# Cosine attention with a gated two-product tail: squares and norms of the next pairs reordered, one activation table load, weights in four transfers, both products of a batch in one phase

## The chip, the cores and the metric

One core of a Trainium2 chip. The time is device microseconds of one launch, the median of several runs; the profile is one execution of the same program, and its span is 1.7 to 1.8 us shorter than the time of that execution.

## The reference, cut to what matters

```python
# q, k, v: (8, 12, 448, 64) fp32; w_in (768, 2048), w_out (2048, 768)
q_n = q / (norm(q) + 1e-6);  k_n = k / (norm(k) + 1e-6)
attn = softmax(q_n @ k_n.T / tau)
x = (attn @ v) laid out as (8 * 448, 768)        # heads side by side
h = x @ w_in
g = h * clip(h + 3, 0, 6) / 6
out = g @ w_out                                  # (3584, 768) fp32
```

## The kernel before: the parts that matter

Heads are worked in 48 pairs, six pairs to a batch. A stretch of six pairs, from slot 2 of pair 6 on, is called a phase: in it the products of finished batches are spread between the attention of the next. A unit, or block, is a group of matmuls into one PSUM bank, up to its eviction, the copy that empties the bank. Each pair has four slots; in a slot TensorE computes scores of two key blocks (one in slot 3), ScalarE takes the exponential, and other work is placed between. The order in this text is the order on each engine's queue.

```python
def norms(i):                          # before: reduction and norms together
    nc.vector.tensor_reduce(out=n2, in_=sq, ...)            # 14 sums of 64 squares
    nc.scalar.activation(out=ln, in_=n2, func=AF.Ln)        # four steps of 128x14
    nc.scalar.activation(out=nr, in_=ln, func=AF.Exp, scale=0.5)
    nc.scalar.activation(out=le, in_=nr, func=AF.Ln, bias=eps_bias)
    nc.scalar.activation(out=r, in_=le, func=AF.Exp, scale=-1.0)

def mm1_unit(b, fc):                   # one block of x @ w_in: 6 matmuls of 448 columns
    ...                                # then ScalarE: u = relu(h/6 + 0.5); VectorE: g = min(u, 1) * h
def mm2_unit(b, t, m):                 # one block of g @ w_out: 16 matmuls of 384 columns
    ...                                # then one copy and the store
def back(i):                           # transposes of a pair's output into Z, VectorE copies Z to xT
    ...
def transposes(i):                     # transposes of normalised q and k into the same Z,
    ...                                # VectorE copies them to qT and kz

def add_batch(b):                      # w_in of batch b, interleaved with w_out of batch b-1
    first = [mm1_unit(b, fc) for fc in range(16)] if b < B else []
    second = [mm2_unit(b - 1, t, m) ...] if b > 0 else []
    ...

for i in range(48):
    for s in range(4):
        if i % 6 == 0 and i > 0 and s == 2:
            add_batch(i // 6 - 1)      # from here six pairs' worth of slots to spread it over
        scores(i, s, SC2 if i < 6 and s % 2 else SC)        # and their exponential
        if s == 0:
            load(...)                  # q, k, v of two pairs
            square(i + 3, nc.gpsimd); normalise(i + 2, nc.gpsimd); vcast(i + 2, nc.gpsimd)
            next_weights()             # one of eight transfers, GpSimd's queue, fp32 to bf16
            fill(0.6 * ns); values(i - 1, 3); finish_values(i - 1); fill(0.4 * ns)
        elif s == 1:
            fill(0.8 * ns); back(i - 1); norms(i + 3); fill(0.2 * ns)
        elif s == 2:
            fill(0.4 * ns); transposes(i + 1); fill(0.6 * ns); values(i, 0); values(i, 1)
        else:
            fill(ns); values(i, 2)
...
add_batch(B - 1); add_batch(B); fill(1e9)      # the tail: w_in of batch 7, w_out of 6 and 7
```

`fill` hands TensorE about that much time of the stream of w_in and w_out units. From pair 6 on, one bank pair (SC) serves all four slots, so the scores of a slot wait for the exponential of the slot before.

Of the kernel before, what the change touches and what calls it, by code (L numbers as in the profile page):

```python
# [8 lines left out]
FP32 = mybir.dt.float32  # L9
BF16 = mybir.dt.bfloat16  # L10
AF = mybir.ActivationFunctionType
ALU = mybir.AluOpType
# [3 lines left out]
MM1_NS = 190.0  # L16
# [4 lines left out]
def kernel(  # L21
# [54 lines left out]
    raw_of, nrm_of, r_of, qT_of, at_of, on_of = {}, {}, {}, {}, {}, {}  # L76


    def load(d, n_pairs=2, first=0, engs=None):

        b, h = 2 * d // HP, 4 * d % H + 2 * first
        if first == 0:
            raw_of[d] = sb.tile([128, 4, 7, D], FP32, name="raw", tag="raw", bufs=3)
        raw = raw_of[d][:, 2 * first : 2 * (first + n_pairs), :, :]
        vt = vr[d % NV][:, 2 * first : 2 * (first + n_pairs), :, :]
        hs = slice(h, h + 2 * n_pairs)
        e0, e1 = engs or (nc.sync, nc.sync)

        def main(t):
            return t[b, hs, 0:SM, :].rearrange("h (p c) d -> p h c d", c=3)  # L90


        for n, t in enumerate((k, q) if b % 2 else (q, k)):
            e0.dma_start(out=raw[:, :, 4 * n : 4 * n + 3, :], in_=main(t))
            e1.dma_start(  # L95
                out=raw[64 * n : 64 * n + 64, :, 3, :],
                in_=t[b, hs, SM:S, :].rearrange("h p d -> p h d"),
            )
        e1.dma_start(out=vt[:, :, 0:3, :], in_=main(v))
        for g in range(2):  # L100
            e0.dma_start(
                out=vt[64 * g : 64 * g + 64, :, 3, :].rearrange("p (i g) d -> p i g d", g=2)[:, :, g, :],
                in_=v[b, hs, SM:S, :].rearrange("(i g) p d -> p i g d", g=2)[:, :, g, :],
            )
# [4 lines left out]
    def square(i, eng):  # L109
        sq = sb.tile([128, 2, 7, D], FP32, name="sq", tag="sq", bufs=2)  # L110
        r_of[i] = sq
        a = raw_pair(i)
        if eng is None:
            nc.scalar.activation(out=sq[:, :, 0:3, :], in_=a[:, :, 0:3, :], func=AF.Square)
            nc.vector.tensor_tensor(
                out=sq[:, :, 3:7, :], in0=a[:, :, 3:7, :], in1=a[:, :, 3:7, :], op=ALU.mult
            )
        else:
            eng.tensor_tensor(out=sq[:, :, :, :], in0=a, in1=a, op=ALU.mult)  # L119

    def norms(i):

        sq = r_of[i]
        n2 = sb.tile([128, 14], FP32, name="n2", tag="n2", bufs=2)
# [4 lines left out]
        nc.vector.tensor_reduce(  # L129
            out=n2[:, :], in_=sq[:, :, :, :].rearrange("p h s d -> p (h s) d"), axis=AX.X, op=ALU.add  # L130
        )
# [191 lines left out]
    def add_batch(b):  # L323

        first = [mm1_unit(b, fc) for fc in range(FCN)] if b < B else []
        second = []
        if b > 0:
            p = b - 1
            second = [mm2_unit(p, t, m) for t in range(3 + p % 2) for m in range(2)]
        stream_ns[0] += len(first) * CC * MM1_NS + len(second) * FCN * MM2_NS  # L330
        done = 0
        for n, u in enumerate(first):
            stream.append(u)
            while second and done * len(first) < (n + 1) * (6 + 2 * ((b - 1) % 2)) - len(first):
                stream.append(second.pop(0))
                done += 1
        stream.extend(second)
# [5 lines left out]
    load(0, 1, 0, (nc.sync, nc.scalar))  # L343
    load(0, 1, 1, (nc.sync, nc.scalar))
    nc.scalar.preload_act_table_set("natural_log_exp_and_others")
    load(1)
    load(2)
# [3 lines left out]
    nc.gpsimd.memset(kz[0][:, :, :], 0.0)  # L351
    for t in vx:
# [4 lines left out]
    nc.gpsimd.memset(kz[1][:, :, :], 0.0)  # L357

    FG = d_ff // 4
    weights = [  # L360
        (w_in_sb[:, :, f * FG : (f + 1) * FG], w_in_r[:, :, f * FG : (f + 1) * FG]) for f in range(4)
    ] + [(w_out_sb[:, 4 * f : 4 * f + 4, :], w_out_r[:, 4 * f : 4 * f + 4, :]) for f in range(4)]

    def next_weights():
        if weights:
            o, w = weights.pop(0)
            nc.gpsimd.dma_start(out=o, in_=w)

    square(0, None)
    norms(0)  # L370
    square(1, nc.vector)
    normalise(0, nc.vector)
    vcast(0, nc.gpsimd)
    norms(1)
    transposes(0)
    normalise(1, nc.vector)
    square(2, nc.gpsimd)
    vcast(1, nc.gpsimd)
    next_weights()
    norms(2)  # L380
# [8 lines left out]
    for i in range(NP):  # L389
# [7 lines left out]
        for s in range(4):  # L397
# [6 lines left out]
            if s == 0:  # L404
                if i % 2 and (i + 5) // 2 < NP // 2:
                    load((i + 5) // 2)
                if i + 3 < NP:
                    square(i + 3, nc.gpsimd)
                if i + 2 < NP:
                    normalise(i + 2, nc.gpsimd)  # L410
                    vcast(i + 2, nc.gpsimd)
                next_weights()
# [5 lines left out]
            elif s == 1:  # L418
                fill(0.8 * ns)
                if i > 0:  # L420
                    back(i - 1)
                if i + 3 < NP:
                    norms(i + 3)
                fill(0.2 * ns)
            elif s == 2:
                fill(0.4 * ns)
# [5 lines left out]
            else:  # L432
                fill(ns)
# [7 lines left out]
    add_batch(B)  # L441
# [36 lines left out]
```

## Time and profile before

| | before |
|---|---|
| median of runs | 510.05 us (509.06 to 512.22) |
| profiled span | 509.7 us, last matmul ends 505.3 |
| exponential of pair 0, slot 0 | 17.39 us |
| exponential of pair 6, slot 2 (start of the stream) | 56.41 us |
| TensorE stalls from there on (see below) | 38.6 us |

In profile lines PE is TensorE, PEld its weight loads, ACT ScalarE, DVE VectorE, POOL GpSimd, SPq and the like the queues that issue transfers. A line of a timeline has start and length in us, engine, line of the kernel and operation; what stands in brackets is how long the engine had been idle and who ended that. SC is the bank pair of the scores, M and Y banks of the products, Z the one bank of all transposes.

A stall here is the start of a matmul less the start of the one before it and that one's streaming time, where over 0.06 us. The page of the profile, parts 2 and 4: busy tenths of 40 equal slices, and the engines' shares of the chain of work that ended last.

```profile
PE   0666767779999999999999999999999999999996
DMA  7999994210432504514432505514431000010022
PE 60%; ACT 15%; DVE 10%; DMA 7%; SPq 4%; issue 2%; POOL 1%; ACTq 0%; POOLq 0%
```

TensorE is below 80% in the first nine slices, DMA at 90% or more in slices two to six; 40% of the chain is not TensorE. The waits, in the form "engine, tile and line waited for whom: us in total, times, longest":

```profile
ACT ln L132 <- DVE n L129: 86.8, 48, 4.4
PE SC L184 <- ACT at L188: 28.4, 36, 3.4
PE Z L154 <- DVE xT L241: 1.7, 3, 0.7
```

The first norm step waits for the reduction in every one of 48 pairs, 86.8 us in total; score products wait for exponentials, 28.4 us.

### The profile page before, as it was taken

To read this page: it belongs to the slowest core of one execution; us is meant where nothing else is said; L and a number is where in the kernel's file an instruction comes from. 1 tells how busy PE (TensorE), PEld (TensorE's weight loads), DVE (VectorE), ACT (ScalarE), POOL (GpSimd) and SP (SyncE) were. 2 spreads that over 40 slices of the span, in tenths; PEclk is the share of its full clock that TensorE was granted. 3 is DMA by queue.
4 is the path that set the end of the run, shared out by engine and by line. 5 is a ranking of instruction groups with operands and counts; after the bars stand their busy time and mean duration, and the time that the engine had idled before them with its cause. 6 is when DMAs were issued, how large, how long until landed. Compare 5 with 4: busy or idle time off the path is not lost.

```text
span 509.7 us, 9679 instructions
## 1 busy us (share of the span) xinstructions
PE 449.6 (88%) x3872; PEld 274.9 (54%) x3872; DVE 259.3 (51%) x568; ACT 282.5 (55%) x543; POOL 189.3 (37%) x156
## 2 busy tenths in 40 slices
PE   0666767779999999999999999999999999999996
PEld 0343434445555656655555656655555656655563
DVE  5665545554645555554645555545645454433310
ACT  3566646666566655566566655566565655533300
POOL 2996275444344343344354343344353320000000
PEclk9988989999999999999999999999999999999999
DMA  7999994210432504514432505514431000010022
GB/s 211 251 221 221 239 221 110 68 41 17 125 97 60 140 15 140 140 39 120 125 90 66 141 18 139 141 36 120 125 107 50 32 27 21 32 48 32 31 78 63
DMA packets 71581, 50.96 MB, mean 100 GB/s; under 512 B 22384, under 2 KB 71536, under 8 KB 71536
## 3 DMA queue, kind: packets, MB, share of 16 engines
q1 hardware_dynamic: 65168, 43.53, 31.5%
q0 software_dynamic: 5248, 6.29, 7.0%
q8 instruction: 30, 0.49, 0.4%
q10 hardware_dynamic: 1120, 0.52, 0.4%
q14 instruction: 15, 0.12, 0.1%
HBM read 45.61 MB, written 11.01 MB: 111 GB/s over the span
## 4 chain that ended last, share of the span: by engine, by line
PE 60%; ACT 15%; DVE 10%; DMA 7%; SPq 4%; issue 2%; POOL 1%; ACTq 0%; POOLq 0%
PE M L286 17%; PE M L257 13%; PE SC L184 9%; PE Y L286 8%; ACT at L188 7%; PE Y L257 7%; DVE n L129 6%; DMA raw<-in_q_dram 5%; PE PV L214 4%; ACT le L134 2%; DVE xT L241 2%; PE Z L240 2%; SPq L95 1%; ACT u L267 1%; ACT nr L133 1%
## 5 line engine op out<-in xcount | busy, mean ns | idle before, releaser
L188 ACT ACTIVATE at<-SC 128x896 bf16<-128x896 f32 x192 | 156.4, 820 | 65.2 <-PE SC L184 63.7
L141 POOL TENSOR_TENSOR nrm<-raw,r 128x896 bf16<-128x896 f32 x46 | 77.6, 1687 | 206.9 <-ACT r L135 196.5
L184 PE MATMUL SC<-qT,kz 128*128 128x448 bf16 x336 | 97.9, 363 | 29.7 <-ACT at L188 28.4
L257 PE MATMUL M<-xT,w_in_sb 128*128 128x448 bf16 x510 | 120.8, 353 | 0.0
L286 PE MATMUL M<-w_out_sb,gT 128*128 128x384 bf16 x608 | 118.1, 326 | 0.0
L286 PEld LDWEIGHTS <-gT 128*128 128x128 bf16 x896 | 84.5, 98 | 60.2 <-issue 5.2
L257 PEld LDWEIGHTS <-w_in_sb 128*128 128x128 bf16 x768 | 72.5, 98 | 77.3 <-issue 22.1
L270 DVE SCALAR_TENSOR_TENSOR gT<-u,M 128x448 bf16<-128x448 bf16 x85 | 52.7, 621 | 98.3 <-ACT u L267 97.9
L119 POOL TENSOR_TENSOR sq<-raw 128x896 f32<-128x896 f32 x46 | 77.3, 1680 | 18.7 <-DMA raw<-in_q_dram 12.2
L214 PEld LDWEIGHTS <-at 128*128 128x128 bf16 x1344 | 64.0, 99 | 30.8 <-ACT at L188 9.3
L214 PE MATMUL PV<-vx,at 128*128 128x65 bf16 (+1 forms) x1344 | 71.7, 199 | 7.0 <-ACT at L188 6.9
L267 ACT ACTIVATE u<-M,half_bias 128x448 bf16<-128x448 f32 x85 | 53.4, 630 | 22.6 <-PE M L257 22.3
L257 PE MATMUL Y<-xT,w_in_sb 128*128 128x448 bf16 x258 | 63.1, 355 | 0.0
L132 ACT ACTIVATE ln<-n 128x14 f32<-128x14 f32 x48 | 10.3, 215 | 86.8 <-DVE n L129 86.8
L286 PE MATMUL Y<-w_out_sb,gT 128*128 128x384 bf16 x288 | 56.7, 326 | 0.0
L129 DVE TENSOR_REDUCE n<-sq 128x14 f32<-128x896 f32 x48 | 51.6, 1076 | 6.7 <-POOL sq L119 4.5
L270 DVE SCALAR_TENSOR_TENSOR gT<-u,Y 128x448 bf16<-128x448 bf16 x43 | 26.7, 621 | 46.3 <-ACT u L267 45.9
L184 PEld LDWEIGHTS <-kz 128*128 128x128 bf16 x336 | 29.7, 99 | 21.3 <-issue 7.9
L154 PE MATMUL Z<-ident,nrm 128*128 128x128 bf16 x336 | 27.9, 225 | 13.4 <-DVE nrm L141 11.4
L154 PEld LDWEIGHTS <-nrm 128*128 128x128 bf16 x336 | 23.9, 101 | 23.5 <-DVE nrm L141 11.4
L229 DVE TENSOR_TENSOR on<-PV,rc 128x512 bf16<-128x512 f32 x48 | 33.2, 691 | 1.7
L241 DVE COPY xT<-Z 128x448 bf16<-128x448 bf16 x48 | 18.7, 389 | 29.1 <-PE Z L240 29.1
(44 smaller groups left out, 244.7 us busy)
## 6 DMA issues: line engine op xcount, KB each, us to landing
out_dram<-o SPq DMA_DIRECT2D x48, 192.0 KB, 1.9
raw<-in_q_dram SPq DMA_DIRECT2D x23, 384.0 KB, 5.1
raw<-in_k_dram SPq DMA_DIRECT2D x23, 384.0 KB, 5.2
vr<-in_v_dram SPq DMA_DIRECT2D x23, 384.0 KB, 5.5
w_in_sb<-in_moe_w_in_dram POOLq DMA_DIRECT2D x4, 768.0 KB, 11.7
w_out_sb<-in_moe_w_out_dram POOLq DMA_DIRECT2D x4, 768.0 KB, 12.2
out_dram<-o SPq DMA_DIRECT2D x16, 96.0 KB, 2.2
raw<-in_q_dram SPq DMA_DIRECT2D x23, 64.0 KB, 4.8
```

The lines of the kernel that those rows point to most:

```text
L119: eng.tensor_tensor(out=sq[:, :, :, :], in0=a, in1=a, op=ALU.mult)
L129: nc.vector.tensor_reduce(out=n2[:, :], in_=sq[:, :, :, :].rearrange("p h s d -> p (h s) d"), axis=AX.X, op=ALU.add)
L141: eng.tensor_tensor(out=nrm[:, :, :, :].rearrange("p s h d -> p h s d"), in0=raw_pair(i), in1=r_of[i][:, :].rearrange("p (h s) -> p h s", ...
L154: nc.tensor.transpose(Z[:, s * 128 : (s + 1) * 128], nrm[:, s, :, :], ident[:, :])
L184: nc.tensor.matmul(sc[:, n, 0:S], k_block(i, name), qT_of[i][:, :], start=True, stop=True)
L188: nc.scalar.activation(out=at[:, 0:m, :], in_=sc[:, 0:m, 0:S], func=AF.Exp, scale=inv_tau)
L214: nc.tensor.matmul(o, at[:, n, q_cols(i // HP, j)], mv, start=(name == "A0" and j % 2 == 0), stop=last, skip_group_check=True,)
L229: nc.vector.tensor_tensor(out=on[:, :, :, :].rearrange("p (b j) h d -> p b (j h) d", b=2), in0=pv4[:, :, :, 0:D], in1=rc[:, :, :].to_broad ...
L257: nc.tensor.matmul(ps[:, 0:S], w_in_sb[:, cc, fc * 128 : (fc + 1) * 128], x[:, cc, c0 : c0 + S], start=(cc == 0), stop=(cc == CC - 1),)
L267: nc.scalar.activation(out=u[:, :], in_=ps[:, 0:S], func=AF.Relu, bias=half_bias[:, :], scale=1.0 / 6.0)
L270: nc.vector.scalar_tensor_tensor(out=g[:, fc, c0 : c0 + S], in0=u[:, :], scalar=1.0, in1=ps[:, 0:S], op0=ALU.min, op1=ALU.mult,)
L286: nc.tensor.matmul(ps[:, 0:MH], lhs, w_out_sb[:, fc, m * MH : (m + 1) * MH], start=(fc == 0), stop=(fc == FCN - 1),)
```

## The change

Its intent: take the norms out of the way by preparing them a slot earlier, start the first pairs sooner (squares shared with ScalarE, loads of q and k ahead of v, no second table load), use fewer weight transfers, and fill the first phase, which had no w_out products. Core of the diff, cut:

```diff
-    def norms(i):                     # reduction and four steps
+    def reduce(i): ...                # the reduction alone
+    def norms(i): ...                 # the four steps alone
...
     def add_batch(b):
-        first = [mm1_unit(b, fc) for fc in range(FCN)] if b < B else []
-        ...                           # w_out of b - 1 interleaved
+        for fc in range(FCN):
+            stream.append(mm1_unit(b, fc))
+        for t in range(3 + b % 2):
+            for m in range(2):
+                stream.append(mm2_unit(b, t, m))
...
-    nc.scalar.preload_act_table_set("natural_log_exp_and_others")   # the second one
-    load(1); load(2)
+    load_qk(1); load_v(0); load_qk(2); load_v(1); load_v(2)
...
-    weights = [4 quarters of w_in] + [4 quarters of w_out]
+    weights = [2 halves of w_in] + [2 halves of w_out]
...
             if s == 0:
-                square(i + 3, nc.gpsimd); normalise(i + 2, ...); vcast(i + 2, ...)
-                next_weights()
             elif s == 1:
+                norms(i + 2)
                 fill(0.8 * ns)
                 back(i - 1)
-                norms(i + 3)
             elif s == 2:
+                square(i + 3, 3 if i < HP else 0, nc.gpsimd)   # 3 of 7 blocks on ScalarE
+                normalise(i + 2, ...); vcast(i + 2, ...)
+                if i in (0, 3, 5): next_weights()
             else:
+                reduce(i + 3)
...
-    add_batch(B - 1); add_batch(B)
+    add_batch(B - 1)
```

More of the change, by code (lines that the diff above doesn't have):

```diff
@@ L74, with load_qk @@
     moe_banks = [Y]
-    raw_of, nrm_of, r_of, qT_of, at_of, on_of = {}, {}, {}, {}, {}, {}
-    def load(d, n_pairs=2, first=0, engs=None):
+    raw_of, sq_of, n2_of, nrm_of, r_of, qT_of, at_of, on_of = {}, {}, {}, {}, {}, {}, {}, {}
+    def load_qk(d, first=0, n_pairs=2, e0=nc.sync, e1=nc.sync):
         b, h = 2 * d // HP, 4 * d % H + 2 * first
@@ L84, in load @@
         raw = raw_of[d][:, 2 * first : 2 * (first + n_pairs), :, :]
-        vt = vr[d % NV][:, 2 * first : 2 * (first + n_pairs), :, :]
         hs = slice(h, h + 2 * n_pairs)
-        e0, e1 = engs or (nc.sync, nc.sync)
-        def main(t):
-            return t[b, hs, 0:SM, :].rearrange("h (p c) d -> p h c d", c=3)
         for n, t in enumerate((k, q) if b % 2 else (q, k)):
-            e0.dma_start(out=raw[:, :, 4 * n : 4 * n + 3, :], in_=main(t))
+            e0.dma_start(
+                out=raw[:, :, 4 * n : 4 * n + 3, :],
+                in_=t[b, hs, 0:SM, :].rearrange("h (p c) d -> p h c d", c=3),
+            )
             e1.dma_start(
@@ L98, in load, with load_v @@
             )
-        e1.dma_start(out=vt[:, :, 0:3, :], in_=main(v))
+    def load_v(d):
+        b, h = 2 * d // HP, 4 * d % H
+        vt, vs = vr[d % NV], v[b, h : h + 4]
+        nc.sync.dma_start(
+            out=vt[:, :, 0:3, :], in_=vs[:, 0:SM, :].rearrange("h (p c) d -> p h c d", c=3)
+        )
         for g in range(2):
-            e0.dma_start(
-                out=vt[64 * g : 64 * g + 64, :, 3, :].rearrange("p (i g) d -> p i g d", g=2)[:, :, g, :],
-                in_=v[b, hs, SM:S, :].rearrange("(i g) p d -> p i g d", g=2)[:, :, g, :],
+            nc.sync.dma_start(
+                out=vt[64 * g : 64 * g + 64, g:4:2, 3, :],
+                in_=vs[g:4:2, SM:S, :].rearrange("h p d -> p h d"),
             )
@@ L107, in raw_pair, with square, reduce @@
         return raw_of[i // 2][:, 2 * (i % 2) : 2 * (i % 2) + 2, :, :]
-    def square(i, eng):
+    def square(i, n_act, eng):
         sq = sb.tile([128, 2, 7, D], FP32, name="sq", tag="sq", bufs=2)
-        r_of[i] = sq
+        sq_of[i] = sq
         a = raw_pair(i)
-        if eng is None:
-            nc.scalar.activation(out=sq[:, :, 0:3, :], in_=a[:, :, 0:3, :], func=AF.Square)
-            nc.vector.tensor_tensor(
-                out=sq[:, :, 3:7, :], in0=a[:, :, 3:7, :], in1=a[:, :, 3:7, :], op=ALU.mult
-            )
-        else:
-            eng.tensor_tensor(out=sq[:, :, :, :], in0=a, in1=a, op=ALU.mult)
+        if n_act:
+            nc.scalar.activation(
+                out=sq[:, :, 0:n_act, :], in_=a[:, :, 0:n_act, :], func=AF.Square
+            )
+        if n_act < 7:
+            eng.tensor_tensor(
+                out=sq[:, :, n_act:7, :], in0=a[:, :, n_act:7, :], in1=a[:, :, n_act:7, :], op=ALU.mult
+            )
+    def reduce(i):
+        n2 = sb.tile([128, 14], FP32, name="n2", tag="n2", bufs=3)
+        n2_of[i] = n2
+        nc.vector.tensor_reduce(
+            out=n2[:, :],
+            in_=sq_of.pop(i)[:, :, :, :].rearrange("p h s d -> p (h s) d"),
+            axis=AX.X,
+            op=ALU.add,
+        )
     def norms(i):
-        sq = r_of[i]
-        n2 = sb.tile([128, 14], FP32, name="n2", tag="n2", bufs=2)
+        n2 = n2_of.pop(i)
         ln = sb.tile([128, 14], FP32, name="ln", tag="ln", bufs=2)
@@ L128, in norms @@
         r = sb.tile([128, 14], FP32, name="r", tag="r", bufs=3)
-        nc.vector.tensor_reduce(
-            out=n2[:, :], in_=sq[:, :, :, :].rearrange("p h s d -> p (h s) d"), axis=AX.X, op=ALU.add
-        )
         nc.scalar.activation(out=ln[:, :], in_=n2[:, :], func=AF.Ln)
@@ L323, in add_batch @@
     def add_batch(b):
-        first = [mm1_unit(b, fc) for fc in range(FCN)] if b < B else []
-        second = []
-        if b > 0:
-            p = b - 1
-            second = [mm2_unit(p, t, m) for t in range(3 + p % 2) for m in range(2)]
-        stream_ns[0] += len(first) * CC * MM1_NS + len(second) * FCN * MM2_NS
-        done = 0
-        for n, u in enumerate(first):
-            stream.append(u)
-            while second and done * len(first) < (n + 1) * (6 + 2 * ((b - 1) % 2)) - len(first):
-                stream.append(second.pop(0))
-                done += 1
-        stream.extend(second)
+        for fc in range(FCN):
[3 more added lines that the diff above has]
+                stream.append(mm2_unit(b, t, m))
+        stream_ns[0] += FCN * CC * MM1_NS + (3 + b % 2) * 2 * FCN * MM2_NS
     for t in vr:
@@ L342 @@
         nc.vector.memset(t[0:64, 1:4:2, 3, :], 0.0)
-    load(0, 1, 0, (nc.sync, nc.scalar))
-    load(0, 1, 1, (nc.sync, nc.scalar))
-    nc.scalar.preload_act_table_set("natural_log_exp_and_others")
-    load(1)
-    load(2)
+    load_qk(0, 0, 1, nc.sync, nc.scalar)
+    load_qk(0, 1, 1, nc.sync, nc.scalar)
+    load_qk(1)
+    load_v(0)
+    load_qk(2)
+    load_v(1)
+    load_v(2)
     nc.vector.memset(eps_bias, EPS)
@@ L350 @@
     make_identity(nc, ident)
-    nc.gpsimd.memset(kz[0][:, :, :], 0.0)
     for t in vx:
@@ L356 @@
         nc.vector.memset(t[64:128, 1, 3, D : D + 1], 1.0)
-    nc.gpsimd.memset(kz[1][:, :, :], 0.0)
-    FG = d_ff // 4
-    weights = [
-        (w_in_sb[:, :, f * FG : (f + 1) * FG], w_in_r[:, :, f * FG : (f + 1) * FG]) for f in range(4)
-    ] + [(w_out_sb[:, 4 * f : 4 * f + 4, :], w_out_r[:, 4 * f : 4 * f + 4, :]) for f in range(4)]
+    for t in kz:
+        nc.gpsimd.memset(t[:, :, :], 0.0)
+    weights = []
+    for f in range(2):
+        c = slice(f * d_ff // 2, (f + 1) * d_ff // 2)
+        weights.append((w_in_sb[:, :, c], w_in_r[:, :, c]))
+    for f in range(2):
+        c = slice(f * FCN // 2, (f + 1) * FCN // 2)
+        weights.append((w_out_sb[:, c, :], w_out_r[:, c, :]))
     def next_weights():
-        if weights:
-            o, w = weights.pop(0)
-            nc.gpsimd.dma_start(out=o, in_=w)
-    square(0, None)
+        o, w = weights.pop(0)
+        nc.gpsimd.dma_start(out=o, in_=w)
+    square(0, 3, nc.vector)
+    reduce(0)
     norms(0)
-    square(1, nc.vector)
+    square(1, 4, nc.gpsimd)
+    reduce(1)
     normalise(0, nc.vector)
+    transposes(0)
+    norms(1)
     vcast(0, nc.gpsimd)
-    norms(1)
-    transposes(0)
-    normalise(1, nc.vector)
-    square(2, nc.gpsimd)
+    square(2, 4, nc.gpsimd)
+    normalise(1, nc.gpsimd)
     vcast(1, nc.gpsimd)
     next_weights()
-    norms(2)
+    reduce(2)
     startup = ExitStack()
@@ L405 @@
                 if i % 2 and (i + 5) // 2 < NP // 2:
-                    load((i + 5) // 2)
-                if i + 3 < NP:
-                    square(i + 3, nc.gpsimd)
-                if i + 2 < NP:
-                    normalise(i + 2, nc.gpsimd)
-                    vcast(i + 2, nc.gpsimd)
-                next_weights()
+                    load_qk((i + 5) // 2)
+                    load_v((i + 5) // 2)
                 fill(0.6 * ns)
@@ L418 @@
             elif s == 1:
+                if i + 2 < NP:
+                    norms(i + 2)
                 fill(0.8 * ns)
@@ L421 @@
                     back(i - 1)
-                if i + 3 < NP:
-                    norms(i + 3)
                 fill(0.2 * ns)
             elif s == 2:
+                if i + 3 < NP:
+                    square(i + 3, 3 if i < HP else 0, nc.gpsimd)
+                if i + 2 < NP:
+                    normalise(i + 2, nc.gpsimd)
+                    vcast(i + 2, nc.gpsimd)
+                if i in (0, 3, 5):
+                    next_weights()
                 fill(0.4 * ns)
@@ L432 @@
             else:
+                if i + 3 < NP:
+                    reduce(i + 3)
                 fill(ns)
@@ L440 @@
     add_batch(B - 1)
-    add_batch(B)
     fill(1e9)
```

## The prediction

> **What bounds the kernel now.** I read the page's slices first, then the busy times in stretches cut at the stages, then who waited for whom, then the timeline where waits repeat. 48 head pairs are processed; each has four slots (score product, exponential, some of the rest). Pairs 0 to 5 run without products of the second part. From slot 2 of pair 6 (the exponential at 56.4 us) a stream of w_in and w_out products fills TensorE. Stretches are cut at slot 2 of pairs 6, 12, 18 and so on.
>
> ```profile
> core 0: us, PE busy (x) PEld busy (x) DVE busy (x) ACT busy (x) POOL busy (x), PEclk, DMA share, GB/s
> 0.00:11.40 11.40, 0.00 (x0) 0.00 (x0) 5.62 (x29) 4.04 (x7) 2.88 (x9) 1.00 0.74 206
> 11.40:56.40 45.00, 28.73 (x301) 17.97 (x302) 26.44 (x58) 28.13 (x62) 36.81 (x31) 0.92 1.17 234
> 56.40:112.50 56.10, 41.82 (x393) 24.48 (x391) 29.98 (x68) 32.85 (x66) 24.87 (x19) 0.97 0.54 130
> 112.50:167.80 55.30, 51.99 (x456) 31.87 (x454) 30.88 (x67) 34.46 (x69) 23.29 (x18) 1.00 0.25 69
> 167.80:226.80 59.00, 57.12 (x505) 35.68 (x504) 31.71 (x69) 35.03 (x69) 23.28 (x18) 1.00 0.35 98
> ...
> 430.00:509.70 79.70, 75.29 (x501) 44.13 (x499) 22.88 (x43) 23.86 (x38) 0.00 (x0) 1.00 0.14 45
> ```
>
> From 112 us on, TensorE is the bound: busy 94 to 97% of each batch. Up to 56 us it is not (64%), and there the DMA share is above 1: transfers of two queues overlap in time on saturated engines. In the first stretch with products, 56 to 112 us, TensorE is busy only 75%: that stretch has w_in products of batch 0 and no w_out product, because w_out runs a batch late.
>
> Busy time counts overlap, so I also took each matmul's start, less the previous matmul's start and its streaming time (the spacing inside runs: 0.189 us for 448 columns, 0.162 for 384), and summed what exceeds 0.06 us. That gives 20.0 us of stalls in 56.4 to 112.5 and 18.6 from there to 430 (2.8 to 4.3 per batch), none after. All but 0.3 us of the 18.6 stand in front of one instruction, the score product of slot 3. One of them, pair 25:
>
> ```profile
> 234.06 1.07 DVE L129 TENSOR_REDUCE n<-sq 128x14 f32<-128x896 f32 x1
> ...
> 235.16 0.21 ACT L132 ACTIVATE ln<-n 128x14 f32<-128x14 f32 x1 [1.92 <-DVE n L129]
> ...
> 236.06 0.21 ACT L135 ACTIVATE r<-le 128x14 f32<-128x14 f32 x1
> ...
> 236.42 0.48 ACT L298 COPY o<-Y 128x384 f32<-128x384 f32 x1
> 236.79 0.92 ACT L188 ACTIVATE at<-SC 128x896 bf16<-128x896 f32 x1
> ...
> 237.77 0.35 PE L184 MATMUL SC<-qT,kz 128*128 128x448 bf16 x1 [0.84 <-ACT at L188]
> ```
>
> The reader is to see ScalarE idle 1.92 us with its queue blocked on VectorE's reduction, then running four small norm steps (235.16 to 236.27), an eviction, and only then the exponential of slot 2, whose scores had been ready since about 234.6. TensorE wants that bank for slot 3 and waits. The norms are not the work of this pair: they serve a pair three later. They merely stand in front.
>
> The second fact is about loading:
>
> ```profile
> 63.64 1.67 POOL L119 TENSOR_TENSOR sq<-raw 128x896 f32<-128x896 f32 x1 [8.02 <-DMA raw<-in_q_dram]
> ```
> ```profile
> 66.46 0.21 ACT L132 ACTIVATE ln<-n 128x14 f32<-128x14 f32 x1 [4.36 <-DVE n L129]
> ```
>
> The squares of pair 10 wait 8 us for q, and ScalarE, in order behind them, 4.4 us. By the packet records the input queue moved 2.37 MB from 9 to 18 us (263 GB/s, alone) but 3.62 MB from 21 to 63 us (86 GB/s), when the weight queue moved 5.90 MB. So an input MB costs 3.8 us and a weight MB (42 - 3.62 x 3.8) / 5.90 = 4.8 us.
>
> **What the Trainium skill says.** "DMA: Bandwidth & Descriptors", Issuing engines are not separate DMA queues: transfers issued by different engines run on the same 16 DMA engines and interleave; the drop from 263 to 86 GB/s agrees. Same page, Queues, rings and completion order: an engine alternates between queues packet by packet. If weight packets grow (below), inputs could get less per turn; no trace here shows it yet. "ScalarE: Activation LUTs", What ACT_TABLE_LOAD costs: about 1283 ns whichever set; here each of the two loads took 1.28 us, so agreed. "Trainium Kernel Development and Optimization", Performance Expectations: matmul busy time is a bad metric as matmuls are pipelined; agreed (a run of four shows 0.92 us where one shows 0.35), hence my spacing count.
>
> **The change, part by part.**
>
> *Both products in one phase.* Total work is unchanged: 6 blocks of w_out of batch 0 (6 x 16 x 0.162 = 15.6 us) move from the end, where TensorE never waits, into 56 to 112 us. Every phase gets the load that the next phases have now (6 or 8 blocks), so that stretch becomes TensorE-bound like them. Worth: the stalls that are there, up to 20 us less what stays. Against it: in a phase, the 16 w_in units now come first, together. Now a pair holds about 3 units; after, 5 to 5.7. Each needs 0.63 us on ScalarE and 0.62 on VectorE. ScalarE's load in such a pair: exponentials 3 x 0.92 + 0.54 = 3.3, norms 1.1, 5.5 x 0.6 = 3.3, sum 7.7 of about 9.3 us. VectorE: reduction 1.08, copies 1.28, output scaling 0.9, xT 0.39, 5.5 x 0.62 = 3.4, sum 7.0. Both fit, but at 75 to 83% with three banks I allow 1 us of stalls per phase, 7 us in all.
>
> *Norms a slot later.* The reduction goes to slot 3, the norms to slot 1 of the next pair, right behind that slot's exponential, with input ready three slots ahead of the old order's need. Per pair ScalarE no longer waits; the four steps end at about 2.6 us after slot 1 begins, and slot 2 is 2.9 us long on TensorE (16 value products and 7 transposes), which covers the delayed exponential. I expect the 0.5 us per pair of slot 3 to go down to 0.1: 18.6 becomes 3, and the same in the first phase.
>
> *Start.* The second table load (at 6.25 us) and two DMA issues leave ScalarE, so the first square starts with its data near 5.2 us, not 7.54. But the reduction of pair 1 now stands ahead of pair 0's normalisation, so that stays near 10 us (10.30 now). The gain comes after: norms of pair 2 no longer precede the first exponential, which moves from 17.39 to about 14. In the pairs of the start, the chain reduction, norms, exponential (5.7 us a pair) opens; ScalarE has 3.3 + 1.1 + a square of 0.52 = 4.9 us of work, so about 5.1 us a pair. Free running, slot 2 of pair 6 would come near 48 us.
>
> *Loads and weights.* Bytes are the same. q and k of pairs 8 and 9 need 6.42 MB of inputs landed: 6.42 x 3.8 + w_in 3.15 x 4.8 + 2 us of start = 41.5, and then they share with the first half of w_out (issued in pair 3): about 48 to 49 us. The square of pair 8 in slot 2 of pair 5 needs them, and now stands in ScalarE's queue too. So the start is held by DMA: slot 2 of pair 5 at about 48.5 (50.42 now), slot 2 of pair 6 at about 53. q and k of pairs 10 and 11: 7.80 x 3.8 + 6.29 x 4.8 + 2 = 62 us, as now (63.5), but needed near 64 and not 55, as the squares come two slots later and the phase is full. That stall shrinks to about 2 us.
>
> *Sum.* From 56.4 to 509.7 are 453.3 us: 38.6 stalls, 4.4 of tail after the last product (505.3), 410.3 the rest, which stays. After: 53 (start) + 410.3 + stalls 7 + 3 + 2 = 12 + tail 4.4 = 479.7 of span. The median is 0.9 above the profiled span: 480.6, about 481 us, 5.8% less. Of the 30 us some 26.6 are stalls of the phases, 3.4 the start.
>
> **The rivals.** (a) *The dense w_in units become the bound*: norms, exponentials and evictions queue up, the stalls move from slot 3 to the products for want of a bank. For it: doubled rate of evictions per pair in half of each phase. Against: today's bank stalls are 0.8 us in all, and the sums leave 17%. It would leave only the 15.6 us of moved work and lose some: 490 to 500. (b) *The start stays DMA-bound or worsens*: w_in goes in two transfers that are both queued by 20 us, where now a quarter goes per pair, and rows of 1024 values instead of 512 may take a larger share of each turn. Inputs of pairs 6 and 7 could then arrive at 36 us, not 29, and stall slot 2 of pair 3 for 4 us. But then the weights are done sooner and give it back; the total of bytes sets the end of the start. It would make slot 2 of pair 6 56 to 57, the time 485. (c) *Everything hides*: the start runs freely at 5 us a pair and phases stall nowhere: 48 + 410 + 5 + 4 = 467.
>
> **Range and chances.** (a) and (b) in part together give 493, a mild (c) gives 472: 472 to 493 for 8 in 10. Moving work into a stretch with 20 us of stalls is nearly arithmetic, so 2% (10 us) is very likely: faster 0.95, within 2% 0.04, slower 0.01.
>
> **What would show it.** First exponential near 14 us; slot 2 of pair 6 at 50 to 56; 75% busy in the first phase up to at least 92%; waits of ScalarE's first norm step on the reduction nearly gone (86.8 us now); score products waiting for the exponential well under the 28.4 us of now; the last stretch shorter by one batch of w_out products. I am wrong if w_in products wait for banks by over 2 us a phase, if ScalarE's squares wait for q or k by over 8 us in all, or if slot 3 still waits.

## More of the kernel before

Line numbers move: exponential L188 to L199, score product L184 to L195, norm steps L132-L135 to L143-L146, transposes L154 to L165, transposes back L240 to L251, xT copy L241 to L252, w_in units L257 to L268, their evictions L267 and L270 to L278 and L281. The reduction stays L129.

## The result, and the profile after

488.21 us median (487.43 to 492.93) against 510.05: ratio 0.9576, 95% interval 0.9512 to 0.9640. A ratio here is always the mean time of one kernel's runs over that of the other's runs of the same rounds, so it is not quite the ratio of the medians. Executions over 1.5% slower than the fastest of the same kernel are left out of the means. Forecast were 481 us and a range of 472 to 493.

The profiled execution is the slowest of its runs (492.93 us, span 491.2, last matmul ends 486.3). Page, parts 2 and 4, after:

```profile
PE   0764599999999999999999999999999999999996
DMA  7999990055403462054402553055401600010012
PE 74%; ACT 9%; DMA 5%; DVE 4%; SPq 3%; POOL 2%; issue 1%; ACTq 0%; POOLq 0%
```

TensorE is at 90% from the sixth slice on, and its share of the chain rises from 60 to 74%. Busy time in stretches cut as before at slot 2 of pairs 6, 12, 18 and 24 (columns as in the prediction's table):

```profile
55.60:111.50 55.90, 53.57 (x471) 33.04 (x470) 31.40 (x67) 34.92 (x67) 24.49 (x19) 0.97 0.49 121
111.50:169.60 58.10, 56.59 (x501) 35.45 (x500) 31.88 (x69) 35.11 (x70) 23.28 (x18) 1.00 0.38 100
169.60:223.90 54.30, 51.96 (x471) 32.28 (x469) 31.66 (x68) 34.92 (x69) 23.28 (x18) 1.00 0.36 99
```

The first phase takes as long as before (55.9 against 56.1 us) with 96 more matmuls of w_out in it, TensorE 96% busy. But the third stretch, with the same load as the second of before (96 w_in and 96 w_out matmuls, 55.3 us there), is only 1 us shorter. The waits of the whole execution show why:

```profile
PE Z L251 <- DVE on L240: 16.4, 6, 9.2
PE Z L165 <- DVE xT L252: 14.2, 18, 1.2
ACT ln L143 <- DVE n L129: 11.2, 4, 7.2
PE SC L195 <- ACT at L199: 0.8, 2, 0.5
```

The old waits are gone (86.8 to 11.2 us, 28.4 to 0.8 us). A wait that was 1.7 us now takes 14.2: the first transpose of slot 2 waits for VectorE's copy of xT. One of the 18, pair 25:

```profile
231.44 0.92 ACT L199 ACTIVATE at<-SC 128x896 bf16<-128x896 f32 x1 [0.81 <-PE SC L195]
232.25 0.21 ACT L143 ACTIVATE ln<-n 128x14 f32<-128x14 f32 x1
...
232.56 0.39 PE L251 MATMUL Z<-ident,on 128*128 128x128 bf16 x4
...
233.13 0.22 ACT L146 ACTIVATE r<-le 128x14 f32<-128x14 f32 x1
...
233.25 1.14 ACT L278 ACTIVATE u<-M,half_bias 128x448 bf16<-128x448 f32 x2
...
233.91 1.15 DVE L281 SCALAR_TENSOR_TENSOR gT<-u,M 128x448 bf16<-128x448 bf16 x2 [1.78 <-ACT u L278]
...
234.97 0.38 DVE L252 COPY xT<-Z 128x448 bf16<-128x448 bf16 x1
...
235.41 0.55 PE L165 MATMUL Z<-ident,nrm 128*128 128x128 bf16 x7 [0.95 <-DVE xT L252]
```

Read it backwards. The transposes (235.41) need Z, which the xT copy (234.97) has to empty. The data of that copy were in Z since 232.95, but in VectorE's queue two evictions of w_in units (233.91) stand ahead of it. They wait for ScalarE's two relu steps (233.25), and these stand behind the four norm steps (232.25 to 233.35). Here the norms themselves wait for nothing. They still stand in front of something.

The start, GpSimd, VectorE and TensorE around 51 us:

```profile
51.04 1.04 POOL L122 TENSOR_TENSOR sq<-raw 128x512 f32<-128x512 f32 x1 [9.84 <-DMA raw<-in_q_dram]
...
52.11 1.09 DVE L129 TENSOR_REDUCE n<-sq 128x14 f32<-128x896 f32 x1 [8.88 <-POOL sq L122]
...
53.47 0.69 DVE L240 TENSOR_TENSOR on<-PV,rc 128x512 bf16<-128x512 f32 x1
...
54.22 0.61 PE L251 MATMUL Z<-ident,on 128*128 128x128 bf16 x4 [9.17 <-DVE on L240]
```

The first four pairs ran at 4.7 to 4.8 us each (5.05 to 5.9 before) and got to slot 3 of pair 5 by 43 us. There the reduction for pair 8 stands at the head of VectorE's queue, waits for squares that wait for q, and holds back the scaling of pair 5's output behind it: TensorE stands for 9.2 us. The start's gain shrinks to 0.8 us in this execution.

### The profile page after: what moved, and what is told of

The parts are those of the page before. It is cut to its first block, busy times and chain, and to the rows that moved or that the text cites. A ratio compares the mean times of both kernels' runs of the same rounds, so it can differ in the third digit from the quotient of the medians.

```text
span 491.2 us, 9737 instructions
## 1 busy us (share of the span) xinstructions
PE 442.0 (90%) x3872; PEld 272.1 (55%) x3872; DVE 258.7 (53%) x566; ACT 286.8 (58%) x550; POOL 183.3 (37%) x154
## 3 DMA queue, kind: packets, MB, share of 16 engines
q1 hardware_dynamic: 65664, 43.92, 32.6%
## 4 chain that ended last, share of the span: by engine, by line
PE 74%; ACT 9%; DMA 5%; DVE 4%; SPq 3%; POOL 2%; issue 1%; ACTq 0%; POOLq 0%
PE M L297 19%; PE M L268 15%; PE Y L297 10%; PE SC L195 9%; PE PV L225 8%; PE Y L268 7%; DMA raw<-in_q_dram 5%; PE Z L165 4%; ACT at L199 3%; ACT u L278 3%; DVE gT L281 3%; SPq L92 1%; PE Z L251 1%; SPq L88 1%; ACT le L145 1%
## 5 line engine op out<-in xcount | busy, mean ns | idle before, releaser
L199 ACT ACTIVATE at<-SC 128x896 bf16<-128x896 f32 x192 | 157.0, 822 | 107.3 <-PE SC L195 105.1
L152 POOL TENSOR_TENSOR nrm<-raw,r 128x896 bf16<-128x896 f32 x47 | 79.3, 1688 | 217.4 <-ACT r L146 202.3
L268 PE MATMUL M<-xT,w_in_sb 128*128 128x448 bf16 x516 | 118.1, 355 | 0.0
L297 PE MATMUL M<-w_out_sb,gT 128*128 128x384 bf16 x592 | 115.1, 326 | 0.0
L268 PEld LDWEIGHTS <-w_in_sb 128*128 128x128 bf16 x768 | 72.5, 98 | 58.5 <-issue 1.3
L195 PE MATMUL SC<-qT,kz 128*128 128x448 bf16 x336 | 96.2, 357 | 1.6 <-DVE qT L179 0.8
L122 POOL TENSOR_TENSOR sq<-raw 128x896 f32<-128x896 f32 (+2 forms) x47 | 73.4, 1562 | 18.3 <-DMA raw<-in_q_dram 9.8
L281 DVE SCALAR_TENSOR_TENSOR gT<-u,M 128x448 bf16<-128x448 bf16 x86 | 53.2, 620 | 50.8 <-ACT u L278 50.0
L278 ACT ACTIVATE u<-M,half_bias 128x448 bf16<-128x448 f32 x86 | 54.0, 630 | 31.8 <-PE M L268 31.7
L225 PE MATMUL PV<-vx,at 128*128 128x65 bf16 (+1 forms) x1344 | 70.6, 198 | 0.4 <-ACT at L199 0.3
L297 PE MATMUL Y<-w_out_sb,gT 128*128 128x384 bf16 x304 | 60.2, 326 | 0.0
L268 PE MATMUL Y<-xT,w_in_sb 128*128 128x448 bf16 x252 | 59.9, 352 | 0.0
L129 DVE TENSOR_REDUCE n<-sq 128x14 f32<-128x896 f32 x48 | 52.0, 1083 | 13.9 <-POOL sq L122 11.1
L165 PE MATMUL Z<-ident,nrm 128*128 128x128 bf16 x336 | 27.7, 224 | 25.9 <-DVE xT L252 14.2
L165 PEld LDWEIGHTS <-nrm 128*128 128x128 bf16 x336 | 23.5, 100 | 37.9 <-issue 20.9
L281 DVE SCALAR_TENSOR_TENSOR gT<-u,Y 128x448 bf16<-128x448 bf16 x42 | 26.0, 620 | 24.6 <-ACT u L278 24.0
L195 PEld LDWEIGHTS <-kz 128*128 128x128 bf16 x336 | 29.3, 98 | 15.1 <-issue 3.0
L239 DVE RECIPROCAL rc<-PV 128x8 f32<-128x8 f32 x48 | 9.8, 205 | 50.9 <-PE PV L225 50.7
L278 ACT ACTIVATE u<-Y,half_bias 128x448 bf16<-128x448 f32 x42 | 26.4, 630 | 14.6 <-PE Y L268 14.6
L240 DVE TENSOR_TENSOR on<-PV,rc 128x512 bf16<-128x512 f32 x48 | 33.2, 692 | 1.7
## 6 DMA issues: line engine op xcount, KB each, us to landing
w_in_sb<-in_moe_w_in_dram POOLq DMA_DIRECT2D x2, 1536.0 KB, 17.1
```

The lines of the kernel that those rows point to most:

```text
L122: eng.tensor_tensor(out=sq[:, :, n_act:7, :], in0=a[:, :, n_act:7, :], in1=a[:, :, n_act:7, :], op=ALU.mult)
L129: nc.vector.tensor_reduce(out=n2[:, :], in_=sq_of.pop(i)[:, :, :, :].rearrange("p h s d -> p (h s) d"), axis=AX.X, op=ALU.add,)
L152: eng.tensor_tensor(out=nrm[:, :, :, :].rearrange("p s h d -> p h s d"), in0=raw_pair(i), in1=r_of[i][:, :].rearrange("p (h s) -> p h s", ...
L165: nc.tensor.transpose(Z[:, s * 128 : (s + 1) * 128], nrm[:, s, :, :], ident[:, :])
L195: nc.tensor.matmul(sc[:, n, 0:S], k_block(i, name), qT_of[i][:, :], start=True, stop=True)
L199: nc.scalar.activation(out=at[:, 0:m, :], in_=sc[:, 0:m, 0:S], func=AF.Exp, scale=inv_tau)
```

## The experiments

"Stalls" are counted as above from each run's own trace, here from the first score product of slot 2 of pair 6 on, and phases are cut there too. That is 0.6 to 1.7 us ahead of the exponential of that slot, which is meant where the time of slot 2 of pair 6 is given, and which cuts the stretches in the parts above and the table of sums below. The changed kernel has 17.3 us of stalls in front of the transposes of slot 2, 1.2 in front of w_in products (at half clock just behind the start, where they follow each other at 0.37 us and not 0.19), and 0.2 each in front of score products and transposes back.

### 1. The changed kernel again

No edit.

> The changed kernel once more, unaltered. Its profiled execution had 10.2 us of half clock (48.3 to 58.6 us) and took 492.9 us where four others took 486.7 to 488.5. Theory: the half clock falls in the wait for q and costs 2 to 4 us of that one execution; here 486 to 489 us, slot 2 of pair 6 again at 53 to 56 us. Rival: the profiled execution is typical and the start is a matter of luck: slot 2 of pair 6 moves by more than 3 us between executions.

Measured: 487.08 us (486.55 to 488.28), ratio 0.9544. Slot 2 of pair 6 at 51.2 us instead of 55.6, span 485.2, 17.1 us of stalls in front of the transposes, every phase from pair 12 on equal to within 0.1 us. So the start differs between executions, by over 3 us, as the rival says, and the first phase behind it by 1.4 us; the time of the first profiled execution is also not typical, as the theory says. Which pair waits for q varies too:

```profile
35.51 1.04 POOL L122 TENSOR_TENSOR sq<-raw 128x512 f32<-128x512 f32 x1 [7.05 <-DMA raw<-in_q_dram]
```

Here the 7 us wait is that for pair 6, and pair 8 waits 1.2 us more. In the first execution GpSimd stood idle for 4.4 us before pair 6 (the profile names a copy of VectorE that ended then) and waited 9.8 us for pair 8.

The clock belongs to this. The granted clock was one half from 48.3 to 58.6 us in the first trace (10.24 us) and from 36.3 to 43.1 us here (6.8 us): it drops about 3 us after TensorE falls idle in the wait for q (at 45.1 and 33.5 us) and comes back 4.3 to 4.4 us after it resumes. The Trainium skill ("TensorE: Matmul & The Clock Gate", Part 1: The HAM clock gate) says that TensorE's clock is gated to half after an idle window of about 3.4 us and released after a busy one; all half-clock stretches in the first 75 us of the traces here are 3.4, 6.8, 10.2 or 13.7 us long, which agrees. A wait in the start thus cost more than its length: the products behind it ran at half clock.

### 2. The phase part alone, on the kernel before

```diff
--- the kernel before
     def add_batch(b): ...             # as changed: w_in, then w_out of the same batch
-    add_batch(B)
```

> The kernel before with one part alone: both products of a batch in one phase. If the moved 15.6 us of w_out products fill idle time of the first phase and nothing else changes: the norms still stand in front of slot 3 (4 to 5 us of stalls a phase), the first phase keeps its 4 us wait for q, so 495 to 499 us. If the norms in their old place and the dense w_in units hinder each other: over 502 us. If the order of the norms were the main cause of the gain: 506 us or more.

Measured: 503.10 us (502.16 to 506.05), ratio 0.9869, 95% interval 0.9827 to 0.9912. Of 15.6 us of moved work only 7.6 us came out: it is the middle case, over 502. The stalls in front of slot 3 stay and grow in the later phases with 6 blocks of w_out (5.2 us each, 4.1 to 4.6 in the kernel before); score products have 28.6 us of stalls in all.

```profile
ACT ln L132 <- DVE n L129: 85.9, 48, 4.0
PE SC L184 <- ACT at L188: 26.3, 35, 4.4
```

Same waits as before the change: the phase part leaves them.

### 3. All but the phase part

```diff
--- the changed kernel
     def add_batch(b): ...             # as before: w_out of batch b - 1 interleaved
     add_batch(B - 1)
+    add_batch(B)
```

> The changed kernel with w_out a batch later again, interleaved with w_in as before; norms, start and weights as changed. If the phase is worth about 13 us: 498 to 503 us. The stalls in front of the first transpose (17.6 us in the changed kernel from 55 us on) tell two theories apart: if they come from the dense w_in units of a phase, they go to under 5 us here; if from the norms standing ahead of slot 1's evictions, over 10 us stay although w_in units come at half the rate.

Measured: 490.42 us (488.94 to 492.45), ratio 0.9607. The time was below the expectation: without the phase part the kernel is only 3.3 us slower than the changed one of the same rounds. The stalls in front of the transposes are 9.3 us, between the two theories; but 3.7 of these lie in the first phase, and the later phases with 6 w_out blocks have none at all and take 51.4 us, where the changed kernel's take 54.1 to 54.4. So the density of w_in units plays a part, and whether it needs the norms to do harm stays open until experiment 5.

How 15.6 us came to 3.3: the first phase took 51.2 us without the w_out blocks and 54.5 with them (experiment 1), so 12.3 us are gained there. From then to the end, the kernel without the phase part took 387.2 us and the changed one 380.4, 6.8 us less and not 15.6: 8.8 us are given back. The start differed by 0.5 us the other way.

### 4. w_out later

```diff
--- the changed kernel
-                if i in (0, 3, 5):
+                if i in (0, 6, 7):
                     next_weights()
```

> The changed kernel with the two w_out transfers issued in pairs 6 and 7 instead of 3 and 5. Theory: the start is held by q of pairs 8 and 9, which share the engines with the first w_out half (51.0 us). By bytes they would land at 6.42 x 3.8 + 3.15 x 4.8 + 2 = 41.5 us, so the 9 us wait vanishes: slot 2 of pair 6 at 46 to 48 us, 479 to 483 us. Rival: the total of bytes only moves the wait to the squares of pair 10 in pair 7: 486 to 489 us.

Measured: 486.56 us (483.04 to 487.84), ratio 0.9519 against 0.9544 of the changed kernel in the same rounds: the intervals overlap, so at these numbers no difference in time is shown: the median lies in the rival's range. In the profiled execution (483.04 us) the wait for q fell to 2.4 us and slot 2 of pair 6 came at 47.4 us, as the theory has it, and no wait for q turned up later, though the rival said that one would. Over six runs the time rose from 483 to 488 while the mean granted clock went from 0.994 to between 0.988 and 0.991. Clock and time go together, but which of them follows the other in the unprofiled runs, these numbers do not show.

### 5. Norms in slot 3

```diff
--- the changed kernel
             elif s == 1:
-                norms(i + 2)
             elif s == 2:
-                normalise(i + 2, ...); vcast(i + 2, ...)
             else:
+                norms(i + 2); normalise(i + 2, ...); vcast(i + 2, ...)
                 reduce(i + 3)
```

> The changed kernel with the norms of pair i+2 in slot 3 instead of slot 1 (and the normalising after them); nothing else moved. Theory A: the first transpose waits for VectorE's copy of xT, which stands behind evictions of w_in units, which wait on ScalarE behind the norms of the same slot 1. Then the stalls in front of the transposes (17.1 us after slot 2 of pair 6) go under 5 us, the phases with 6 w_out blocks take about 51.5 us instead of 54.1 to 54.4, and the time is 474 to 479 us. Theory B: the dense evictions alone hold the copy back, wherever the norms stand: over 12 us of these stalls stay, 484 to 488 us.

Measured: 476.08 us (473.69 to 477.37), ratio 0.9298, 95% interval 0.9261 to 0.9334. Stalls in front of the transposes: 1.5 us, all stalls 3.7. Phases with 8 and 6 blocks, busy times as before:

```profile
107.70:164.20 56.50, 56.50 (x502) 35.50 (x500) 31.91 (x68) 35.10 (x68) 23.91 (x19) 1.00 0.38 102
164.20:215.80 51.60, 51.52 (x471) 32.24 (x469) 31.39 (x67) 34.62 (x67) 22.69 (x19) 1.00 0.38 104
```

TensorE is busy almost without a gap, although w_in units are as dense as in the changed kernel. In pair 25 the evictions now follow the exponential and the xT copy is done in time:

```profile
224.14 0.92 ACT L199 ACTIVATE at<-SC 128x896 bf16<-128x896 f32 x1 [0.80 <-PE SC L195]
...
224.95 1.15 ACT L278 ACTIVATE u<-M,half_bias 128x448 bf16<-128x448 f32 x2
...
226.68 0.38 DVE L252 COPY xT<-Z 128x448 bf16<-128x448 bf16 x1
...
227.12 0.55 PE L165 MATMUL Z<-ident,nrm 128*128 128x128 bf16 x7
```

Theory A holds, and B falls: density alone does no harm, norms in slot 1 with dense evictions do. In slot 3 the scores are one block, so the exponential is 0.54 us and leaves room.

### 6. Norms back in their old place

```diff
--- the changed kernel
             if s == 0:
+                square(i + 3, 3 if i < HP else 0, nc.gpsimd)
             elif s == 1:
-                norms(i + 2)
                 fill(0.8 * ns); back(i - 1)
+                reduce(i + 3); norms(i + 3)
             elif s == 2:
-                square(i + 3, ...)
             else:
-                reduce(i + 3)
...
+    norms(2)                          # ahead of the pairs, behind reduce(2)
```

> The changed kernel with squares in slot 0, and reduction and norms of pair i+3 together behind the transposes of slot 1, as before the change; start, weights and phases as changed. Theory: the stalls in front of the score product of slot 3 come back (28.6 us after slot 2 of pair 6 where the phase was changed alone) and replace the 17.1 us in front of the transposes, so it costs 10 to 14 us: 497 to 502 us. If the place of the norms were worth only the start: 487 to 490 us.

Measured: 502.89 us (502.67 to 504.55), ratio 0.9831. The stalls in front of score products are back at 31.0 us (30.1 of them slot 3's) and those of the transposes are 1.3, as expected, only a little dearer. It is within 0.4% of the phase part alone (experiment 2): start, loads and weights as changed give nothing that shows if the norms stay where they were, and the first pairs run at 5.8 us again (27.1 to 32.9 us from pair 2 to 3).

### 7. Eight weight transfers

```diff
--- the changed kernel
-    weights = [2 halves of w_in] + [2 halves of w_out]
+    weights = [4 quarters of w_in] + [4 quarters of w_out]
-                if i in (0, 3, 5):
+                if i < 7:
                     next_weights()
```

> The changed kernel with the weights in eight transfers again, one per pair up to pair 6. Theory: w_in rows of 1024 values give weight packets of 2048 bytes and a larger share of each turn: the input queue moved 51 GB/s beside them (4.46 to 5.23 MB from 21 to 36 us in the run with late w_out), 100 GB/s beside packets of 1024 bytes in the kernel before. With small rows it moves 80 to 100 GB/s again from 21 to 36 us; the wait for q in pair 5 depends on the sum of bytes and stays within 3 us, so 485 to 490 us. Rival: fewer, larger transfers were worth 2% by themselves: 495 us or more.

Measured: 488.13 us (487.73 to 488.86), ratio 0.9536, the changed kernel's value. By the packet records the input queue moved 1.37 MB from 21 to 36 us (91 GB/s) beside weight packets of 1024 bytes; in the changed kernel 0.69 MB (46 GB/s, experiment 1) beside packets of 2048. So larger rows in fewer transfers (the two were changed together) do halve what the inputs get meanwhile. But here pair 6 has its q in time, and pair 8 waits:

```profile
46.22 1.03 POOL L122 TENSOR_TENSOR sq<-raw 128x512 f32<-128x512 f32 x1 [8.39 <-DMA raw<-in_q_dram]
```

The wait changes pairs (7.05 + 1.16 us at pairs 6 and 8 there, 8.39 us at pair 8 here) and in these two executions keeps its sum, as it would if the sum of bytes set it. The first execution of the changed kernel had more (experiment 1), so this is not shown. No worth of fewer transfers shows in the time.

### 8. Norms in slot 3 and w_out later

Experiments 4 and 5 together.

> Norms in slot 3 and w_out in pairs 6 and 7 together, hoped to be the best of all. If both savings add (12 us of transposes' stalls, 2 to 4 us of the start): 470 to 475 us, 0.92 to 0.93 of the kernel before. If the clock takes part of it back, as the runs with late w_out went from 483 to 488 us with the granted clock going from 0.995 to 0.988: 474 to 480 us.

Measured: 470.21 us (468.67 to 474.91), ratio 0.9199, 95% interval 0.9157 to 0.9240. The savings at least add: 6 us below experiment 5 in the same rounds, which shows the gain from late w_out that experiment 4 could not. All stalls 2.5 us.

### 9. The same without the phase part

```diff
--- experiment 8
     def add_batch(b): ...             # as before the change
     add_batch(B - 1)
+    add_batch(B)
```

> The kernel with norms in slot 3 and late w_out, but w_out blocks a batch later again as before the change. Theory: the phase part is worth the idle time of the first phase (10.9 us of stalls between the two changed kernels), and the changed kernel gave most of it back as stalls in front of the transposes; with the norms out of the way nothing is given back, so without the phase part 480 to 484 us against 470.2 with it. Rival: the phase part is worth only the 3 us by which the changed kernel beat its version without it: 472 to 475 us.

Measured: 478.42 us (478.15 to 479.61), ratio 0.9375 against 0.9199. The two are from different rounds: the phase part is worth 8.2 us by the medians, 9.0 by the ratios (0.0176 of 511 us) and 10.5 by the two profiled spans (477.8 and 467.3). The time lies between the two ranges, 1.6 us under the theory's and 3.4 us over the rival's: nearer the theory, and the rival's 3 us are out. Both kernels' later phases are equal now (51.4 to 51.9 and 56.4 to 56.7 us, at most 1.3 us of stalls), so nothing is given back; and the empty first phase takes 46.5 us with 10.5 us of stalls, 51.6 when filled. It had taken 51.2 with the norms in slot 1 (experiment 3), 54.3 in the kernel before, both also with w_out loaded early: the other parts shorten the same stretch that the phase part fills.

### 10. Weights later still

```diff
--- experiment 8
-    next_weights()                    # ahead of the pairs
-                if i in (0, 6, 7):
+                if i in (0, 3, 6, 7):
                     next_weights()
```

> Norms in slot 3, w_out in pairs 6 and 7, and the two w_in transfers in pairs 0 and 3 instead of before the pairs and in pair 0. If the inputs of pairs 6 to 9 still wait for w_in at the start, slot 2 of pair 6 comes at 45 to 47 us instead of 48.5 and the time is 467 to 469 us. If the start is at its own pace by now (4.8 us a pair), 469 to 472 us. If the second half of w_in comes too late for pair 7: over 473 us.

Measured: 467.94 us (466.11 to 468.31), ratio 0.9164, 95% interval 0.9132 to 0.9196: 8.4% below the kernel before, the best of all that was run, 4% below the changed one. Slot 2 of pair 6 came at 46.2 us, so this is the first case: the inputs had still waited for w_in. The six runs lie within 2.2 us, where those of experiment 8 spread over 6.2. The difference in time from experiment 8 is within the intervals.

### 11. Squares of the start on GpSimd alone

```diff
--- the changed kernel
-                    square(i + 3, 3 if i < HP else 0, nc.gpsimd)
+                    square(i + 3, 0, nc.gpsimd)
```

> The changed kernel with the squares of the start's pairs on GpSimd alone again (those of pairs 0 to 2 ahead of the pairs stay shared). Theory: the start's end is set by q of pairs 8 and 9 and not by who squares: 486 to 489 us, within 0.4% of the changed kernel. Rival: the shared squares carry the shorter pairs: 490 us or more.

Measured: 489.02 us (486.42 to 489.85), ratio 0.9575: at the upper edge of the theory's range. Pairs ran at 4.8 to 5.1 us, and slot 2 of pair 6 came at 53.2 us, within the changed kernel's two executions. If sharing the squares is worth anything, it is below what the wait for q varies by.

### 12. The second table load back

```diff
--- the changed kernel
     load_qk(0, 1, 1, nc.sync, nc.scalar)
+    nc.scalar.preload_act_table_set("natural_log_exp_and_others")
```

> The changed kernel with the second table load put back behind ScalarE's DMA issues. Theory: the load delays the first square by about 1.3 us and the first exponential by at most that, but the later wait for q swallows it: 486 to 489 us. Rival: it shifts everything behind it: 488.5 us or more, 1.3 us over the changed kernel of the same rounds.

Measured: 490.71 us over all six runs (486.18 to 494.13); the profiled execution counts as slow (494.13 us, half clock for 13.7 us around the wait for q). The five fast runs have a median of 488.73 us and a ratio of 0.9597 with an interval of 0.9544 to 0.9651, which overlaps that of experiment 1. Both medians are in the rival's range, but the spread is too wide for a verdict on time. The trace of the start is plain, though:

```profile
3.92 1.28 ACT L348 ACT_TABLE_LOAD   x1 [1.90 <-DMA raw<-in_q_dram]
5.21 0.52 ACT L118 ACTIVATE sq<-raw 128x384 f32<-128x384 f32 x1
7.03 0.21 ACT L143 ACTIVATE ln<-n 128x14 f32<-128x14 f32 x1 [1.30 <-DVE n L129]
```

The first square moves from 4.01 to 5.21 us, but the first norm step only from 6.98 to 7.03 (changed kernel, first trace), because the reduction also needs VectorE's part of the squares, which waits for k. The first exponential is at 13.88 us in both (13.35 in experiment 1). Up to there the load was hidden; that it costs nothing in the end is not shown.

### What the parts are worth together

| medians, us | w_out a batch later | both products in one phase |
|---|---|---|
| kernel before, norms after the transposes of slot 1 | 510.7 | 503.1 (exp. 2) |
| changed kernel, norms at the front of slot 1 | 490.4 (exp. 3) | 487.1 (exp. 1) |
| norms in slot 3, w_out weights later | 478.4 (exp. 9) | 470.2 (exp. 8) |

The phase part is worth 7.6, 3.3 and 8.2 us, depending on where the norms stand.

## Why the prediction was right

The time lay in the range, 7 us above the number. The prediction's sum, against both executions of the changed kernel, each term from its own trace:

| term of the sum, us | predicted | profile of the result | experiment 1 |
|---|---|---|---|
| start, to slot 2 of pair 6 | 53 | 55.6 | 51.2 |
| stalls of the phases | 12 | 18.6 | 17.7 |
| tail after the last matmul | 4.4 | 4.9 | 4.8 |
| the rest | 410.3 | 412.1 | 411.5 |
| span | 479.7 | 491.2 | 485.2 |

- *Work is conserved, stalls are what can be had.* Right: the rest was 411.5 to 412.1 us. The larger value has about 3 us of products at half clock in it (55.6 to 58.6 us).
- *Norms a slot later.* Right in its own effect: slot 3's stalls are gone (none counted, 3 allowed), the wait on the reduction fell from 86.8 to 11.2 us. Experiment 6 puts the whole step at 15 us (ratios 0.9831 and 0.9544, from different rounds, times 511).
- *Dense w_in units.* The term that was mis-sized: "I allow 1 us of stalls per phase, 7 us in all", for want of banks. Banks cost at most 0.4 us (experiment 1). 17 us stand in front of the transposes instead, which the prediction did not list. That the total missed by only 7 us is in part luck: the 3 us allowed for slot 3 and the 2 for q of pair 10 did not come. And none of the three signs of being wrong came, for none was set on this path. It had checked that norms in slot 1 do not delay the exponential of slot 2. It did not follow the other queue: norms, relu steps, VectorE's evictions, xT copy, Z. Rival (a) had the right cause, a queue of norms, exponentials and evictions, and the wrong place. Experiments 3 and 5 show that it takes both, dense w_in units and norms in slot 1.
- *Both products in one phase, "up to 20 us less what stays".* Too simple. The other parts also shorten the first phase, and both claimed the same stalls. Alone it gave 7.6 us, on top of the other parts 3.3.
- *Start.* Right in what holds it, the landing of q and k, and in its size between two executions (55.6 and 51.2, forecast 53); the estimate of 48 to 49 us for pairs 8 and 9 met 51.0 in one and 44 in the other. Rival (b) was right too about the share of larger rows: experiment 1 has the q of pair 6 at 35.5 us, where the rival said 36 (32.6 in the first execution). Not right: that ScalarE's square would stand in the way. In pair 5 it waited 0.4 us; the reduction at the head of VectorE's queue did it.
- *First exponential near 14 us, 5.1 us a pair.* 13.88 us, and 4.7 to 4.8 us for the first four pairs.

## What to carry to other kernels

When a side task is taken out of one engine's critical place, follow every queue behind its new place to the end, not only the consumer that suffered before: here the norms left the exponential's way and stood in the evictions' way, and moving them two slots further gained 11 us more by the medians and 12.6 by the ratios, about half as much again as the whole change. Parts that feed on the same idle time do not add; cross them in a table before saying what each is worth. While loads are at the limit of the DMA engines, order them by when they are needed and put weights that are needed late behind inputs that are needed early.

## What the Trainium skill lacked or had wrong

- "DMA: Bandwidth & Descriptors", Queues, rings and completion order, says that an engine alternates between queues packet by packet, but has no figure for what a casting weight stream leaves to plain loads. Here inputs kept 263 GB/s alone (kernel before, from 9 to 18 us), 88 to 93 GB/s beside weight packets of 1024 bytes (kernel before and experiments 2 and 7, from 21 to 36 us) and 46 to 52 GB/s beside packets of 2048 bytes (the changed kernel and its variants with the same w_in halves at the same places).
- "Perfetto Trace Analysis", Optimization Strategy (under Identifying Performance Opportunities), names one possible cause of a gap that repeats on the engine that should be saturated: too little SBUF or PSUM for the next tile. Both repeating gaps here, 0.5 us per pair in front of slot 3's scores before and up to 1.2 us in front of the transposes after, were waits for a single PSUM tile (SC, Z), but four small steps (1.1 us) in an engine's queue ahead of the work that frees it made them. Moving these steps took the stalls of the phases from 18.2 to 3.7 us (experiments 1 and 5) with no buffer added; whether a second tile would have done it too was not run.
